# Small transposing products and one weight's join moved in the opening of a Fourier-mixing and gated feed-forward kernel

## The chip, the cores and the metric

The kernel runs on one core of one Trainium2 chip. The metric is the device time of one execution in microseconds. A core has a matrix engine (TensorE, PE in the profile) and three others that work on whole tiles: VectorE (DVE), ScalarE (ACT) and GpSimd (POOL). SyncE (SP) issues most DMA transfers. Each engine runs its own instructions strictly in order and waits on semaphores for the others.

## The reference

The input x has shape (8, 3008, 256). Its two-dimensional Fourier transform over sequence and features is taken, and the real part, as 24064 rows of 256, goes through a gated feed-forward layer:

```
X = fft(fft(x, axis=1), axis=2).real
gate = sigmoid(X @ w_gate)          # w_gate, w_val: 256 x 1536
out = (gate * (X @ w_val)) @ w_out  # w_out: 1536 x 256
```

The weights arrive as 64-bit floats.

## The kernel before

**Merged weights.** The transform over features is a fixed 256 x 256 matrix of cosines and sines (`dt`), so the kernel multiplies it into the two input weights once: `merge` (L335) makes G = dt x W. G has a cosine half G1 and a sine half G2. Row 0 of G2 is not a sine row but the row of the one middle frequency, and it is needed as a number per partition. So `ge_sums` (L351) transposes that row by products with a one-element matrix, 128 weights at a time, into the columns of one PSUM bank, and ACT copies the columns to `ge` (L360).

**Eighteen jobs.** The weights are cut in 18 jobs of 256 columns or rows. Jobs 0 to 11 alternate between gate and value weights (job 2c is gate, 2c+1 value, of column block c), 12 to 17 are of w_out. Each job is loaded (`weight_load`), its 64-bit numbers are taken apart on ACT (`weight_parts`, L301 and L302), put together as 32-bit numbers with three DVE instructions (L313, L314, L316, with a PSUM bank as scratch) and one POOL addition (L318, `weight_join`), and then used (`weight_use`): for jobs 0 to 11 four products on PE into a bank `ps`, which `merged` (L344) copies to G on ACT.

**Banks.** PSUM has eight banks. Three (`psx`) rotate among the merges of jobs 0 to 7 and the `pf` sums; five (`po0` to `po4`, NB = 5) are named by number through `bank(name, other)`. Whoever takes a bank waits until its last user's reads are done.

**The transform over the sequence.** For each of eight batches, rows are folded (on DVE for batch 0), then products with a cosine and a sine table (`st`) give sums `ev` and `od` of even and odd inputs for two blocks of frequencies. From them `half().then` (L511) copies `ev` to SBUF on ACT, and `places` (L526) writes sum and difference on DVE to the row tiles: `pk` for cosines, `qk` for sines. The sum fills the lower half of the frequencies from the start on, the difference the upper half from the end down. The middle feature's own row (`er`, `e0_sums`, `e0_copies`, `e0_row`) is spread to all partitions as `ek`.

**The main loop.** An iteration i (L1008) handles 128 of the 1536 inner columns for a chunk of 252 frequencies. Its sums lie in a bank `pf`: `seed` (ACT) writes ek x ge, `front_a` (PE) adds G1 x pk, `part` (ACT) copies twice that to `ae`, `front_b` (PE) adds G2 x qk. `gate_a` and `gate_b` (ACT and DVE) make sigmoid and product for a frequency and its mirror. `back` is the product with w_out; for the first chunk it goes straight to `rows` banks, later in a form with fewer products (`po`). Seeds rotate through the three `psx` banks, so a seed waits for the gate of three iterations before.

**The opening.** Ahead of the loop: PE is kept busy with products of ones (`warm`), jobs 0 to 7 are joined and merged, all their ge columns are made in one call (L895), batch 0 is folded and its cosine sums are taken (`cos`), the first three seeds, then jobs 8 and 9 are taken apart and joined (L918), and the sine sums (`sin`) alternate with the first three `front_a`. Jobs 8 to 17 are used inside the loop: the dictionaries `pre`, `mid` and `use` (L951 to L963) give, for each job, the iteration in which it is taken apart, joined and merged, and the iteration after that for its ge columns:

```
    for j, i in ((8, -2), (9, -1), (10, 0), (11, 1), (12, 2), (13, 4), ...
        ...
        use.setdefault(i + 2, []).append(lambda j=j: using(j))
        if jobs[j][0] < 2:
            use.setdefault(i + 3, []).append(lambda j=j: ge_sums((j,), (j + 1) % 2))
```

`using(j)` merges in bank `po` j % 2 and copies G at once. Inside an iteration the order is: front_a, gate_a, part, seed, gate_b (with `mid` in it), `pre`, `use`, back, front_b.

Of the kernel before, what the change touches and what calls it, by code (L numbers as in the profile page):

```python
# [12 lines left out]
ALU = mybir.AluOpType  # L13
# [69 lines left out]
def kernel(  # L83
# [10 lines left out]
    nc = tc.nc  # L94
    B, _, _, _, D = xf.shape
# [3 lines left out]
    M = S // 2  # L99
    NK = M + 1  # L100
    NE = (M // 2) // 2 + 1
    NO = (M // 2) // 2
    NFT = F // P
# [3 lines left out]
    NB = 1 + max(b // 3 for b in PLACE)  # L107
# [22 lines left out]
    op = ctx.enter_context(tc.tile_pool(name="op", bufs=1))  # L130
# [3 lines left out]
    def mm(o, l, r, start, stop):  # L134
        nc.tensor.matmul(o, l, r, start=start, stop=stop, skip_group_check=True)  # L135

    def bank(name, other=None):
        if other is not None:
            return pso.tile([P, 512], F32, name=name, tag=f"po{other}")
        return psx.tile([P, 512], F32, name=name, tag="x")  # L140
# [42 lines left out]
    ST = [const.tile([P, 2, NQ, NE + NO], F32, name="st", tag="st")]  # L183
# [3 lines left out]
    ge = const.tile([P, 2, NFT], F32, name="ge")  # L187
# [57 lines left out]
    jobs = [(w, c) for c in range(NPR) for w in range(2)] + [(2, c) for c in range(NPR)]  # L245
# [50 lines left out]
    def weight_parts(j):  # L296

        if j in RAW:
            raw, ws = RAW[j], WS[j]
            lo, hi = raw[:, :, :, 0], raw[:, :, :, 1]  # L300
            nc.scalar.activation(ws, hi.bitcast(F32), AF.Abs)  # L301
            nc.scalar.activation(lo, lo.bitcast(U32), AF.Copy, scale=2.0 ** -29)  # L302

    def weight_join(j, other=None):
        if j not in RAW:
            return
        raw, ws = RAW.pop(j), WS[j]
        lo, hi = raw[:, :, :, 0], raw[:, :, :, 1]
        wi = ws.bitcast(I32)
        mid_ = ws if other is None else bank("join", other).rearrange("p (c f) -> p c f", c=2)  # L310
        mi = mid_.bitcast(I32)
        ts = nc.vector.tensor_scalar
        ts(out=mid_, in0=ws, scalar1=2.0 ** -15, scalar2=HUGE, op0=ALU.max, op1=ALU.min)  # L313
        ts(out=mi, in0=mi, scalar1=3, scalar2=0x3FFFFFF8, op0=ALU.logical_shift_left,  # L314
           op1=ALU.bitwise_and)
        nc.vector.scalar_tensor_tensor(out=wi, in0=hi, scalar=-(2 ** 30), in1=mi,  # L316
                                       op0=ALU.bitwise_and, op1=ALU.bitwise_or)
        nc.gpsimd.tensor_tensor(wi, wi, lo, op=ALU.add)  # L318
# [3 lines left out]
    def weight_use(j, other=None):  # L322
        w, c = jobs[j]
        if w == 2:
            WO[c] = WS.pop(j)
            if c >= NPR - 2:
                lo = 2 * (c - NPR + 2)
                nc.sync.dma_start(out=wkeep[:, lo : lo + 2], in_=WO[c])
            for g in range(NG):
                if (3 * g + 2) // 2 == c:  # L330
                    parts_.extend(forms(g))
        else:
            merge(WS.pop(j), w, c, other)
# [10 lines left out]
    def merged(j):  # L344

        g, c = jobs[j]
        ps = MERGED.pop((g, c))
        cs = slice(c * WC, (c + 1) * WC)
        nc.scalar.copy(G[:, :, g, cs], ps.rearrange("p (h n) -> p h n", h=2))

    def ge_sums(js, other=None):  # L351

        ps = bank("ge", other)
        at_ = [(jobs[j][0], f) for j in js for f in range(2 * jobs[j][1], 2 * jobs[j][1] + 2)]
        for g, f in at_:
            mm(ps[:, g * NFT + f : g * NFT + f + 1], G2[0:1, g, f * P : (f + 1) * P], busy[0:1, 0:1],
               True, True)
        gs = sorted({g for g, _ in at_})
        lo, hi = min(f for _, f in at_), max(f for _, f in at_) + 1
        nc.scalar.copy(ge[:, gs[0] : gs[-1] + 1, lo:hi],  # L360
                       ps[:, 0 : 2 * NFT].rearrange("p (g f) -> p g f", g=2)[:, gs[0] : gs[-1] + 1, lo:hi])

    def forms(g):

# [122 lines left out]
    def half(b, w, d, blk, sn, other=None):  # L487


        c0, n = ((0, NE), (NE, 2 * NJ if b else NO))[blk]  # L490
        ev, od = [bank(name, other and other[i])[:, 0:n] for i, name in enumerate(("ev", "od"))]

        def sums(*qs):
            for q in sorted(qs, key=lambda q: q % 2):
                mm((ev, od)[q % 2], w(q), ST[0][0:NP, int(sn), q, c0 : c0 + n], q < 2, q >= NQ - 2)

        def both():

            for r in range(2):
                for q in range(N3):  # L500
                    for par, sum_ in enumerate((ev, od)):
                        rows = slice(par * HP, par * HP + HP - 1 - (par and q == N3 - 1))
                        if blk:
                            out_, wq = sum_[:, r * NJ : (r + 1) * NJ], q + N3 * r
                            tab = ST[1][rows, r ^ int(sn), q]
                        else:
                            out_, wq = sum_[:, r::2], q + N3 * (r ^ int(sn))
                            tab = ST[0][rows, int(sn), q, r:NE:2]
                        mm(out_, w(wq)[rows], tab, q == 0 and r == 0, q == N3 - 1)

        def then():  # L511
            a = evp.tile([P, 2 * NJ], F32, name="a", tag="a")
            if b and blk:
                for par, sum_ in enumerate((ev, od)):
                    f = a[:, par * NJ : (par + 1) * NJ]
                    nc.scalar.copy(f, sum_[:, 0:NJ])
                    for r, op_ in enumerate((ALU.add, ALU.subtract)):
                        nc.vector.tensor_tensor(ST[2][:, par, r::2], f[:, r : NJ - 1 + r],
                                                sum_[:, NJ + r : 2 * NJ - 1 + r], op=op_)
                return lambda: places(d, blk, sn, ST[2][:, 0], ST[2][:, 1])  # L520
            a = a[:, 0:n]
            nc.scalar.copy(a, ev)
            return lambda: places(d, blk, sn, a, od)
        return sums, then, both

    def places(d, blk, sn, ev, od):  # L526
        nc.vector.tensor_tensor(d[:, blk : blk + 2 * ev.shape[1] - 1 : 2], ev, od, op=ALU.add)
        lo, hi = (od, ev) if sn else (ev, od)
        top = M - blk
        nc.vector.tensor_tensor(d[:, top : top - 2 * NO + 1 : -2], lo[:, 0:NO], hi[:, 0:NO],  # L530
                                op=ALU.subtract)

    def whole(b, blk, what):
        _, then, both = seq_group(b, blk, what, (2, 3) if what else (0, 1))
# [8 lines left out]
    def seq_group(b, blk, what, other=None):  # L543
        return half(b, lambda q: W[b, blk][what][:, q, :], PQE[b][what], blk, what == 1, other)
# [33 lines left out]
    def e0_spread():  # L578

        ps = bank("ek", NB - 1)[:, 0:CH]  # L580
        mm(ps, busy[0:1, 0:P], shared["er"][:, 0:CH], True, True)
        EK[0] = ekp.tile([P, CH], F32, name="ek", tag="ek")
        nc.scalar.copy(EK[0], ps)
# [295 lines left out]
    def warm(n):  # L879

        ps = bank("warm", NB - 1)
        for _ in range(n):
            mm(ps[:, 0:CH], busy[:, 0:P], busy, True, True)

    shared["er"] = pqp.tile([P, NK + 1], F32, name="er", tag="pk")[0:1]
    warm(14)
    for j in range(8):
        weight_parts(j)
        if j > 2:
            merged(j - 3)  # L890
        weight_join(j, j % NB)
        weight_use(j)
    for j in range(5, 8):
        merged(j)
    ge_sums(range(8), 3)  # L895
    for j in range(N3):
        load_table(1, j)
    for j in range(8, KEEP):
# [11 lines left out]
        for sums, _, _ in cos:  # L910
            sums(2 * j, 2 * j + 1)
    put = [then() for _, then, _ in cos]
    for f in put:
        f()
    e0_spread()
    for i in range(N3):
        seed(i)
    for j in (8, 9):  # L918
        weight_parts(j)
        weight_join(j, NB - 1)  # L920
    sin = [seq_group(0, blk, 1, (2 * blk, 2 * blk + 1)) for blk in range(2)]

    def sines(j):
# [3 lines left out]
    def first(i):  # L927
        front_a(i)
        if i < 2:
            part(i)  # L930
# [3 lines left out]
    first(1)  # L934
    sines(2)
    first(2)
    for _, then, _ in sin:
        then()()
    for j in range(KEEP, len(jobs)):
        weight_load(j)  # L940
    nc.sync.dma_start(out=ed[0:1], in_=shared["er"])
# [9 lines left out]
    pre, use, mid = {}, {}, {}  # L951
    def using(j):
        weight_use(j, j % 2)
        if jobs[j][0] < 2:
            merged(j)
    for j, i in ((8, -2), (9, -1), (10, 0), (11, 1), (12, 2), (13, 4), (14, 6), (15, 8), (16, 10), (17, 12)):
        if i > 0:
            pre.setdefault(i - 1, []).append(lambda j=j: weight_parts(j))
        if i >= 0:
            mid.setdefault(i, []).append(lambda j=j: weight_join(j, 2))  # L960
        use.setdefault(i + 2, []).append(lambda j=j: using(j))
        if jobs[j][0] < 2:
            use.setdefault(i + 3, []).append(lambda j=j: ge_sums((j,), (j + 1) % 2))  # L963


    i0 = NFT
# [123 lines left out]
```

## Time and profile before

| What | Value |
|---|---|
| median of 3 runs | 1943.3 us (1940.19, 1943.3, 1943.42) |
| the profiled execution's own time | 1941.99 us |
| its span | 1940.2 us |
| PE busy | 1923.7 us, 99% of the span |
| DVE, ACT, POOL busy | 74%, 69%, 81% |
| last job joined ahead of the loop's own (job 9, DVE) | 51.67 us |
| first product of `front_b` | 54.80 us |
| first product of `rows` | 78.77 us |

A timeline line gives the start in the span, the time of the group, engine and line of the code, the operation, what it writes and reads, shapes, how many instructions were merged into the line, and in brackets the idle time ahead of it and what ended it. Every product is an instruction of helper line L135, so tiles tell them apart; a product of 32-bit numbers is two records, so four products show as x8. Ends of matmuls are modelled: the start of the next group is the better mark.

### The profile page before, as it was taken

How to read it: one execution, taken by the hardware profiler on the slowest of the kernel's cores; microseconds unless marked ns; L12 is line 12 of the kernel's file. 1: busy time of each engine (PE TensorE's matmuls, PEld its weight loads, DVE VectorE, ACT ScalarE, POOL GpSimd, SP SyncE). 2: the span in 40 equal slices, each digit the busy share in tenths (PEclk: the TensorE clock that was granted, in tenths of full speed). 3: DMA queues.
4: the chain of work that ended last, by engine and by line, in shares of the span. 5: the costliest groups of instructions: out<-in, count | busy, mean ns of one | idle time of the engine just before them, and what ended most of it. 6: DMA issues, size and time to landing. Idle time of an engine off the chain costs nothing.

```text
span 1940.2 us, 34490 instructions
## 1 busy us (share of the span) xinstructions
PE 1923.7 (99%) x11296; PEld 1793.6 (92%) x11296; DVE 1432.2 (74%) x3210; ACT 1347.6 (69%) x3151; POOL 1563.8 (81%) x2806
## 2 busy tenths in 40 slices
PE   9899999999999999999999999999999999999999
PEld 6799889999999999999999999999999999999998
DVE  7556787777777877778777786777777777776776
ACT  4677657776777677776777767777677776777775
POOL 2379989997889788986889878888789886777775
PEclk9999999999999999999999999999999999999999
DMA  9351422212022111312012021111200110011101
GB/s 293 119 109 30 113 60 67 52 23 79 15 52 55 37 57 20 71 31 79 17 35 69 14 81 26 47 47 22 83 17 15 21 21 14 15 19 22 25 17 30
DMA packets 165098, 97.87 MB, mean 50 GB/s; under 512 B 126298, under 2 KB 155068, under 8 KB 163128
## 3 DMA queue, kind: packets, MB, share of 16 engines
q1 hardware_dynamic: 164366, 95.17, 20.4%
q8 instruction: 91, 1.49, 0.3%
q14 instruction: 87, 0.71, 0.1%
q10 hardware_dynamic: 522, 0.50, 0.1%
q0 software_dynamic: 32, 0.00, 0.0%
HBM read 70.40 MB, written 47.24 MB: 61 GB/s over the span
## 4 chain that ended last, share of the span: by engine, by line
PE 95%; DVE 3%; ACT 1%; issue 0%; DMA 0%; POOL 0%; ACTq 0%; DVEq 0%
PE pf L135 49%; PE po L135 40%; PE ev L135 3%; PE rows L135 1%; PE od L135 1%; DVE c L819 1%; PE ps L135 1%; DVE z L679 0%; ACT pf L692 0%; PE row L135 0%; DVE join L314 0%; DVE h L691 0%; DVE h L695 0%; PE pe L135 0%; DVE join L313 0%
## 5 line engine op out<-in xcount | busy, mean ns | idle before, releaser
L701 POOL TENSOR_TENSOR sf<-h 128x168 f32<-128x168 f32 (+1 forms) x935 | 517.9, 573 | 213.1 <-DVE h L695 213.1
L701 POOL TENSOR_TENSOR sf<-h,sf 128x168 f32<-128x168 f32 (+1 forms) x1122 | 625.0, 577 | 58.1 <-DVE h L695 57.8
L135 PE MATMUL pf<-qk,G 128*128 128x252 f32 (+1 forms) x2304 | 583.0, 376 | 2.1 <-ACT ae L664 1.9
L135 PE MATMUL pf<-pk,G 128*128 128x252 f32 (+1 forms) x2304 | 582.8, 376 | 0.0
L695 DVE TENSOR_TENSOR h<-pf,z 128x252 f32<-128x252 f32 (+1 forms) x576 | 241.5, 419 | 428.2 <-ACT pf L692 428.2
L653 ACT ACTIVATE pf<-ek,ge 128x252 f32<-128x252 f32 (+1 forms) x1152 | 542.7, 471 | 18.9
L135 PE MATMUL po<-sf,wf 128*128 128x168 f32 (+1 forms) x2992 | 516.1, 305 | 0.0
L664 ACT ACTIVATE ae<-pf 128x504 f32<-128x504 f32 (+1 forms) x576 | 339.6, 590 | 233.2 <-PE pf L135 231.2
L135 PEld LDWEIGHTS pf<-pk,G 128*128 128x128 f32 x2304 | 436.3, 190 | 53.5 <-issue 1.6
L135 PEld LDWEIGHTS po<-sf,wf 128*128 128x128 f32 x2992 | 460.6, 190 | 8.1
L135 PE MATMUL po<-h,wf 128*128 128x168 f32 (+1 forms) x2618 | 463.2, 305 | 0.0
L819 DVE TENSOR_TENSOR c<-c 128x168 f32<-128x168 f32 (+1 forms) x929 | 437.9, 503 | 5.1
L135 PEld LDWEIGHTS pf<-qk,G 128*128 128x128 f32 x2304 | 410.9, 190 | 29.9 <-ACT ae L664 3.4
L135 PEld LDWEIGHTS po<-h,wf 128*128 128x128 f32 x2618 | 416.5, 190 | 16.2
L679 DVE TENSOR_TENSOR z<-ae,pf 128x504 f32<-128x504 f32 (+1 forms) x576 | 383.4, 666 | 42.1 <-ACT h L678 40.5
L678 ACT ACTIVATE h<-pf 128x252 f32<-128x252 f32 (+1 forms) x576 | 218.0, 378 | 161.8 <-PE pf L135 157.5
L692 ACT ACTIVATE pf<-z 128x252 f32<-128x252 f32 (+1 forms) x576 | 214.1, 372 | 89.0 <-DVE h L691 86.4
L691 DVE TENSOR_TENSOR h<-h,pf 128x252 f32<-128x252 f32 (+1 forms) x576 | 232.5, 404 | 0.0
L701 POOL TENSOR_TENSOR sf<-sf 128x168 f32<-128x168 f32 (+1 forms) x187 | 108.0, 578 | 14.7
L701 POOL TENSOR_TENSOR sf<-sf,h 128x168 f32<-128x168 f32 (+1 forms) x187 | 102.2, 546 | 0.0
L732 ACT COPY c<-po 128x504 f32<-128x504 f32 (+1 forms) x141 | 80.1, 568 | 0.0
L828 DVE STREAM_TRANSPOSE os<-c 128x256 f32<-128x256 f32 x184 | 70.7, 422 | 0.3 <-issue 0.3
(152 smaller groups left out, 919.7 us busy)
## 6 DMA issues: line engine op xcount, KB each, us to landing
x<-xr SPq DMA_DIRECT2D x14, 1536.0 KB
out_dram<-os SPq DMA_DIRECT2D x368, 56.0 KB
xr<-in_xf_dram SPq DMA_DIRECT2D x14, 768.0 KB
xr<-in_xf_dram SPq DMA_DIRECT2D x35, 256.0 KB
ek<-ed SPq DMA_DIRECT2D x39, 126.0 KB
out_dram<-os SPq DMA_DIRECT2D x284, 7.0 KB
st<-in_stab_dram SPq DMA_DIRECT2D x6, 658.9 KB
x<-in_xf_dram SPq DMA_DIRECT2D x3, 1024.0 KB
```

Source lines behind the costliest of these rows:

```text
L135: nc.tensor.matmul(o, l, r, start=start, stop=stop, skip_group_check=True)
L653: nc.scalar.activation(PF[i][:, g], EK[i // NFT], AF.Copy, scale=ge[:, g, f : f + 1])
L664: nc.scalar.activation(AP[i], PF[i], AF.Copy, scale=2.0)
L678: nc.scalar.activation(H[p][:, fh, 0:n], PF[i][:, 0], AF.Sigmoid)
L679: nc.vector.tensor_tensor(z[:, :, ::-1], AP.pop(i), PF[i], op=ALU.subtract)
L691: nc.vector.tensor_tensor(h[:, fh, 0:n], h[:, fh, 0:n], pf[:, 1], op=ALU.mult)
L692: nc.scalar.activation(pf[:, 0], z[:, 0], AF.Sigmoid)
L695: nc.vector.tensor_tensor(h[:, fh, n:], pf[:, 0], z[:, 1], op=ALU.mult)
L701: nc.gpsimd.tensor_tensor(block(p, dst), block(p, a), block(p, b), op=(ALU.subtract, ALU.add)[op])
L732: (nc.vector.tensor_copy if t == 1 or t == 3 and not last else nc.scalar.copy)(C[0][:, 3 * t * R : 3 * (t + 1) * R], PO[t][:, 0 : 3 * R])
L819: engine.tensor_tensor(t[:, dst * R : (dst + 1) * R], *v, op=(ALU.subtract, ALU.add)[op])
L828: nc.vector.transpose(os_[0][:, s, 0:nb, h, :], t[:, c0 : c0 + nb * TB])
```

## The change

Four edits, all in the first 75 us or so:

- `ge_sums` is split: it makes the products into a bank that may be handed in, and a new `ge_out` makes ACT's copy. The ge products of jobs 0 to 5 go into bank po3 one job at a time, between the merges of jobs 3 to 7, with one copy; those of jobs 6 and 7 go to bank po4 in iteration 0, behind the merge of job 8.
- The joins of jobs 0 to 7 use three banks instead of five, and there are 12 warm products instead of 14.
- `places` can do its lower or its upper part alone (argument `high`). For batch 0, both blocks' lower parts come first, then both upper parts. The join of job 9 moves behind all four of the sines' parts; it used to stand ahead of the sine sums.
- In the loop, jobs 8 to 11 are merged in iterations 0, 2, 3, 4 (before: 0, 1, 2, 3), each with its ge one iteration later, in banks po3, po4, po3 and po0 (before: the bank `(j + 1) % 2`, which is the one that the next merge uses).

The order of instructions changes on PE, DVE and ACT. On POOL and SP it stays.

```diff
-    def ge_sums(js, other=None):
-
-        ps = bank("ge", other)
-        at_ = [(jobs[j][0], f) for j in js for f in range(2 * jobs[j][1], 2 * jobs[j][1] + 2)]
-        for g, f in at_:
+    def ge_at(js):
+        return [(jobs[j][0], f) for j in js for f in range(2 * jobs[j][1], 2 * jobs[j][1] + 2)]
+
+    def ge_sums(js, other, ps=None):
+
+        ps = bank("ge", other) if ps is None else ps
+        for g, f in ge_at(js):
             mm(ps[:, g * NFT + f : g * NFT + f + 1], G2[0:1, g, f * P : (f + 1) * P], busy[0:1, 0:1],
                True, True)
...
+        return ps
+
+    def ge_out(js, ps):
+        gs, fs = [sorted({a[i] for a in ge_at(js)}) for i in range(2)]
+        to = slice(gs[0], gs[-1] + 1), slice(fs[0], fs[-1] + 1)
+        nc.scalar.copy(ge[:, to[0], to[1]],
+                       ps[:, 0 : 2 * NFT].rearrange("p (g f) -> p g f", g=2)[:, to[0], to[1]])
...
+    def places(d, blk, sn, ev, od, high=None):
+        if not high:
+            nc.vector.tensor_tensor(d[:, blk : blk + 2 * ev.shape[1] - 1 : 2], ev, od, op=ALU.add)
+        if high in (None, 1):
...
-    warm(14)
+    warm(12)
+    ges = None
     for j in range(8):
         weight_parts(j)
         if j > 2:
             merged(j - 3)
-        weight_join(j, j % NB)
+        weight_join(j, j % 3)
+        if j == 7:
+            merged(5)
+            ge_sums((4, 5), None, ges)
         weight_use(j)
-    for j in range(5, 8):
+        if 2 < j < 7:
+            ges = ge_sums((j - 3,), 3, ges)
+    ge_out(range(6), ges)
+    for j in (6, 7):
         merged(j)
-    ge_sums(range(8), 3)
...
     put = [then() for _, then, _ in cos]
-    for f in put:
-        f()
+    for high in range(2):
+        for f in put:
+            f(high)
...
     for j in (8, 9):
         weight_parts(j)
-        weight_join(j, NB - 1)
+    weight_join(8, NB - 1)
...
-    for _, then, _ in sin:
-        then()()
+    put = [then() for _, then, _ in sin]
+    for high in range(2):
+        for f in put:
+            f(high)
+    weight_join(9, NB - 1)
...
-        use.setdefault(i + 2, []).append(lambda j=j: using(j))
-        if jobs[j][0] < 2:
-            use.setdefault(i + 3, []).append(lambda j=j: ge_sums((j,), (j + 1) % 2))
+        if jobs[j][0] == 2:
+            use.setdefault(i + 2, []).append(lambda j=j: using(j))
+    for j, i, other in ((8, 0, 3), (9, 2, 4), (10, 3, 3), (11, 4, 0)):
+        use.setdefault(i, []).append(lambda j=j: using(j))
+        use.setdefault(i + 1, []).append(lambda j=j, other=other: ge_out((j,), ge_sums((j,), other)))
+    use[0].append(lambda: ge_out((6, 7), ge_sums((6, 7), 4)))
```

More of the change, by code (lines that the diff above doesn't have):

```diff
@@ L349, in merged @@
         nc.scalar.copy(G[:, :, g, cs], ps.rearrange("p (h n) -> p h n", h=2))
-    def ge_sums(js, other=None):
-        ps = bank("ge", other)
-        at_ = [(jobs[j][0], f) for j in js for f in range(2 * jobs[j][1], 2 * jobs[j][1] + 2)]
-        for g, f in at_:
+    def ge_at(js):
[3 more added lines that the diff above has]
+        for g, f in ge_at(js):
             mm(ps[:, g * NFT + f : g * NFT + f + 1], G2[0:1, g, f * P : (f + 1) * P], busy[0:1, 0:1],
                True, True)
[L358 to L361, printed above, removed]
+        return ps
[4 more added lines that the diff above has]
+                       ps[:, 0 : 2 * NFT].rearrange("p (g f) -> p g f", g=2)[:, to[0], to[1]])
     def forms(g):
@@ L519, in then @@
                                                 sum_[:, NJ + r : 2 * NJ - 1 + r], op=op_)
-                return lambda: places(d, blk, sn, ST[2][:, 0], ST[2][:, 1])
+                return lambda *a: places(d, blk, sn, ST[2][:, 0], ST[2][:, 1], *a)
             a = a[:, 0:n]
             nc.scalar.copy(a, ev)
-            return lambda: places(d, blk, sn, a, od)
+            return lambda *b_: places(d, blk, sn, a, od, *b_)
         return sums, then, both
[L526 to L531, printed above, removed]
+    def places(d, blk, sn, ev, od, high=None):
+        if not high:
+            nc.vector.tensor_tensor(d[:, blk : blk + 2 * ev.shape[1] - 1 : 2], ev, od, op=ALU.add)
+        if high in (None, 1):
+            lo, hi = (od, ev) if sn else (ev, od)
+            top = M - blk
+            nc.vector.tensor_tensor(d[:, top : top - 2 * NO + 1 : -2], lo[:, 0:NO], hi[:, 0:NO],
+                                    op=ALU.subtract)
     def whole(b, blk, what):
```

## The prediction

> **What bounds the kernel now.** I read the page's head first, then the chain of waits, then each engine's timeline over the first 80 us, where alone the two instruction orders differ (POOL and SP keep theirs; from the first `rows` product on PE's order is the same too).
>
> ```profile
> span 1940.2 us, 34490 instructions
> PE 95%; DVE 3%; ACT 1%; issue 0%; DMA 0%; POOL 0%; ACTq 0%; DVEq 0%
> ```
>
> PE carries 95% of the chain, so a microsecond that PE gains before `rows` and that nothing later absorbs is a microsecond of the span. PE's timeline (start, us, group, what it waited for):
>
> ```profile
> 26.36 3.73 PE L135 MATMUL ge<-busy,G 1*128 1x1 f32 x32
> 30.02 1.11 PE L135 MATMUL pe<-st,x 126*1 126x377 f32 x8
> ...
> 54.80 1.01 PE L135 MATMUL pf<-qk,G 128*128 128x252 f32 x4
> 55.74 0.60 PE L135 MATMUL ge<-busy,G 1*128 1x1 f32 x4
> 59.21 1.96 PE L135 MATMUL ps<-raw,dt 128*128 128x256 f32 x8 [2.87 <-ACT ge L360]
> 61.01 1.01 PE L135 MATMUL pf<-qk,G 128*128 128x252 f32 x4
> 61.95 0.60 PE L135 MATMUL ge<-busy,G 1*128 1x1 f32 x4
> 64.13 3.37 PE L135 MATMUL ps<-wc,dt 128*128 128x256 f32 x8 [1.58 <-ACT ge L360]
> ...
> 72.60 1.96 PE L135 MATMUL ps<-wc,dt 128*128 128x256 f32 x8 [2.58 <-ACT ge L360]
> ```
>
> There is one solid block of ge products, 3.66 us from its start to the next group's, and later three idle stretches, 2.87 + 1.58 + 2.58 = 7.03 us, each a merge waiting for ACT's copy of the previous ge out of the same bank. `rows` starts at 78.77. ACT's timeline shows the other anchor:
>
> ```profile
> 47.92 0.67 ACT L301 ACTIVATE raw<-raw 128x512 f32<-128x512 f32 x1 [0.18 <-DMA raw<-in_moe_w_val_dram]
> 48.50 0.67 ACT L302 ACTIVATE raw<-raw 128x512 int32<-128x512 uint32 x1
> 49.06 0.57 ACT L664 ACTIVATE ae<-pf 128x504 f32<-128x504 f32 x1
> ```
>
> Weight 9 lands at 47.9, and ACT does nothing behind it earlier. The DMA queue is full until then; the change moves no DMA issue ahead of it.
>
> **The change, step by step.**
>
> *Two warm products fewer, three join banks instead of five: 0.* Warming would end 0.85 us earlier (4 passes of 0.21), but the merges are fed by POOL every 2.06 us, and by the fourth (15.26) PE already waits for POOL. The joins of one bank follow each other on DVE anyway.
>
> *The first ge products between merges: PE 3 us earlier at 27, worth 0 by 50.* Now 4 passes (0.46 by the block's rate, 3.66/32) follow merges 3, 4, 5 and 6, and 8 passes (0.92) come ahead of merge 7. The merges take 1.78 back to back. From merge 3 at 15.26 (1.93 to the next group): 17.2, and with three more pairs of merge and ge 17.65, 19.9, 22.1 to 24.4; ge of jobs 4 and 5 to 25.3; merge 7 to 27.1. POOL's join 7 (end 24.39) is hidden. So the first `pe` starts at 27.1 instead of 30.02. ACT has one copy more (0.17, cover: it idles 2.42 ahead of its last G copy). But the third part of x reaches DVE at 31.80 and its sums are ready at 36.0, so the last cosine group starts at 36.1 instead of 39.35, `ek` at 38.8 instead of 42.07. The reordered cosine places cost here: the sines' first od product waits for the place that frees its bank,
>
> ```profile
> 42.86 0.53 DVE L530 TENSOR_TENSOR pk<-a,od 128x376 f32<-128x376 f32 x1
> ```
>
> which now stands behind the other block's lower one (its copy ends at 39.6): 40.6 instead of 40.0, 0.6 lost. First pf product 42.6 instead of 45.45. Then ACT meets weight 9 at 47.92 as before: `part` at 49.06 and 49.55, the sines' copies at 50.05 and 50.45 (before 50.52 and 51.78, held by PE).
>
> *The sines' places ahead of join 9: +0.7 at the first qk product.* On DVE the join of weight 9 ran from 49.46 to 51.67. Now DVE idles from 49.4 until the copy (50.56), does four places in 1.85, and only then the join: 52.4 to 54.55 (three of 0.73). On POOL its addition is late by as much and passes nothing; join 10 ends at 56.6 instead of 55.55. On PE the last pf of the opening ends at 50.3, merge 8 starts when POOL has weight 8 (50.8; before 53.07) and ends at 52.75. The ge of jobs 6 and 7 is next, and its bank is the one join 9 works in: PE stands idle **1.85 us**, until 54.6. With 0.92 for the eight passes the first qk product starts at 55.5 instead of 54.80. Were join 9 still early, the lower places would end at 53.0 as before and the first qk product, behind ge, could start at 53.7: this part by itself costs 1.8.
>
> *Merges one step earlier, ge in banks of their own: -8 us from there to rows.* From the first qk product to `rows` took 78.77-54.80 = 23.97. PE's work in it is 8 pf groups of 0.85, three merges of 1.78, four ge of 0.46: 14.0. The rest was the 7.03 of waits, 1.7 of a half-clock stretch (below), and 1.2 of refills. Now the merge follows the next qk product and waits for POOL only (56.0, 58.0, 61.5; all hidden), and each ge waits for G copied a step before. What is late next is ACT: h at 56.6, `part` 57.75, sigmoid 58.25, weight 12's two conversions to 59.7, h at 59.75; DVE's second h product of group 0, behind join 11, ends at 60.4; only then may ACT seed the bank again (0.97): 61.45. So the first new pf starts at 61.5 with PE free at 60.35: 1.15 idle. Later the ge of job 10 waits 0.5 for G behind weight 13's conversions. Otherwise PE runs: 62.8 merge 10, 64.6, 65.4, 67.3 merge 11, 69.1, 69.9, ge, `rows` at **71.3**; I add 0.2 for weight loads that the tiny groups expose (0.09 at 55.74). 71.5 against 78.77 is -7.3.
>
> *Clock.* The windows over PE show the granted clock:
>
> ```profile
> 63.00:64.00 1.00, 0.00 (x0) 1.00 0.00 0
> 64.00:65.00 1.00, 0.87 (x3) 0.77 0.00 0
> 65.00:66.00 1.00, 1.00 (x3) 0.50 0.06 16
> 66.00:67.00 1.00, 1.00 (x4) 0.50 0.00 0
> ```
>
> Half clock came twice, 30.4 to 33.8 after the ge block, 64.5 to 67.9 after waits, 3.4 us each; the stretch of 3.4 us before each held at most about a third of dense products. The new stretch 52.75 to 55.5 holds none, so a half-clock stretch after it is likely (2 in 3, since its place varies). It slows 1.8 us of work by double up to 61.5, where 1.15 is idle: about 0.3 of it gets through (0 to 1.7).
>
> [...]
>
> **Sum.** The profiled execution's own time is 1941.99 (its span and 1.8 around it): -7.3 + 0.3 gives **1935.0**. It lies 1.3 below the median of 1943.3, so against that the sum is -0.43%. Bounds: tiny passes at 0.15 (0.60/4) instead of 0.114 in the main loop give +0.4; no new waits (1.85 + 1.15 + 0.5) -3.5, but the seeds tie the second, so -2.4 at most; a full half-clock stretch +1.4; the three runs lie from 1.8 below to 1.4 above that own time.
>
> **Rivals.**
> 1. *ACT takes the place of the waits* (12%). Its seeds, conversions and copies fill each step; if each of the three steps still holds PE by the smallest old wait (1.58 instead of my 1.65 in all), 3 x 1.58 - 1.65 = +3.1: 1938.1. For it: 61.5 is set by ACT. Against: PE's work per step (3.94) is over ACT's 3.7.
> 2. *The waits stay under other names* (8%): the ge products waited for their copy only because ACT came late; G's copy is as late. The sum loses all but the half-clock: 1941.99 + 0.7 - 1.7 = 1941. Against it: the merge was released by the ge copy in all three rows.
> 3. *The late join decides* (6%): join 9 ends 2.9 later (54.55 for 51.67). If joins 10 to 12 and the gates behind them on DVE carry this on, and the old waits remain, the merges are late by 2.9, the eight ge passes in front of the first qk product come on top (0.92), and the longer gap brings another half-clock stretch (1.7): 1941.99 + 5.5 = 1947.5, slower than before. It decides from the point where join 10 (56.6) ends after the first h (57.04): now 0.4 short of it.
> 4. *The clock stays full* (part of the forecast's 74%): 1934.7.
>
> **Chances.** Forecast with or without the half clock 74%, rivals 12, 8, 6. A measurement here tells 0.2%, 3.9 us, from no change; faster means under 1939.4. Forecast and rival 1 lie there, but for 0.03 in their tails: 0.83; same holds rival 2, these tails and a milder rival 3: 0.12; slower the rest of rival 3: 0.05. The range goes from 1931.9 (own time's low run and the waits in part) to 1939.0, past rival 1; it leaves out the rest.
>
> **What would show it.** `pe` at 27 rather than 30; 6 ge copied before the last G; the first qk product near 55.5 behind ge that waited for DVE's join; no `ps` waiting for ACT's ge; `rows` at 71 to 72, and the same duration from there to the end. Wrong if the ge of jobs 6 and 7 is not held by the join (then about 2 less), or if `rows` is later than 75.

## The result and the profile after

| | before | after |
|---|---|---|
| median | 1943.42 us (5 runs, 1940.19 to 1947.12) | 1934.58 us (5 runs, 1934.3 to 1937.33) |
| the profiled execution's own time, its span | 1941.99, 1940.2 us | 1937.33, 1935.5 us |
| first `pe` product | 30.02 us | 27.96 us |
| first qk product | 54.80 us | 55.84 us |
| first `rows` product | 78.77 us | 74.06 us |

The ratio of the times on record is 0.9958, with a 95% interval of 0.9943 to 0.9973: faster by 0.42% (the two medians divided give 0.9955). 1935.0 was predicted. Three executions of one experiment (own banks, below) took 2415, 3393 and 6060 us, the first two at mean granted clocks of 0.78 and 0.56; they are left out.

The profiles place the whole difference ahead of `rows`: it starts 4.71 us earlier, the span is 4.7 shorter. The profiled execution is the slowest of the five after, so this is less than the 8.8 between the medians. This is PE's timeline of the kernel after.

```profile
24.61 1.49 PE L135 MATMUL ge<-busy,G 1*128 1x1 f32 x12
26.04 1.99 PE L135 MATMUL ps<-wf,dt 128*128 128x256 f32 x8
27.96 0.81 PE L135 MATMUL pe<-st,x 126*1 126x377 f32 x8
...
51.10 1.99 PE L135 MATMUL ps<-wf,dt 128*128 128x256 f32 x8 [0.17 <-POOL wf L318]
54.87 1.05 PE L135 MATMUL ge<-busy,G 1*128 1x1 f32 x8 [1.77 <-DVE raw L316]
55.84 1.12 PE L135 MATMUL pf<-qk,G 128*128 128x252 f32 x4
56.89 0.88 PE L135 MATMUL ge<-busy,G 1*128 1x1 f32 x4
57.71 2.05 PE L135 MATMUL pf<-qk,G 128*128 128x252 f32 x4
59.55 3.62 PE L135 MATMUL ps<-raw,dt 128*128 128x256 f32 x8
...
65.75 1.99 PE L135 MATMUL ps<-wc,dt 128*128 128x256 f32 x8
...
69.90 1.99 PE L135 MATMUL ps<-wc,dt 128*128 128x256 f32 x8
...
74.06 1.99 PE L135 MATMUL rows<-wc,h 128*128 128x256 f32 x8
```

The three idle stretches of 2.87, 1.58 and 2.58 ahead of `ps` are gone. In their place stands one wait of 1.77 at the ge products of jobs 6 and 7, on the last DVE instruction of join 9. Merge 9 (59.55) takes 3.62 instead of 1.99: the windows over PE of the same kernel show half clock there (columns: window, length, PE busy and count, granted clock, DMA share, GB/s).

```profile
56.00:57.00 1.00, 1.00 (x5) 1.00 1.05 389
57.00:58.00 1.00, 1.00 (x5) 0.53 0.54 186
...
63.00:64.00 1.00, 1.00 (x4) 0.55 0.00 0
64.00:65.00 1.00, 1.00 (x7) 1.00 0.00 0
```

The granted clock in the rows at 57 and 63 (0.53 and 0.55) puts it from 57.06 to 63.9. The chain of waits of the kernel after, from 30 to 80 us, tells what sets the start of all this:

```profile
35.66 12.45 DMA raw<-in_moe_w_val_dram
...
49.43 0.95 ACT ae L671 x2
50.38 0.37 ACT a L527
...
51.78 0.92 DVE qk L537 x2
52.70 0.61 DVE join L313
...
54.12 0.70 DVE raw L316
54.83 0.04 issue
54.87 1.05 PE ge L135 x8
```

Weight 9's transfer, ACT's two `part` and two copies, DVE's places, join 9, and only then PE. PE's earlier finish of the opening is not on it.

### The profile page after: what moved, and what is told of

Same layout as the page of the kernel before. It is cut to its first block, busy times and chain, and to the rows that moved or that the text cites. A ratio compares the mean times of both kernels' runs of the same rounds, so it can differ in the third digit from the quotient of the medians.

```text
span 1935.5 us, 34483 instructions
## 1 busy us (share of the span) xinstructions
PE 1924.0 (99%) x11292; PEld 1793.3 (93%) x11292; DVE 1435.0 (74%) x3210; ACT 1346.7 (70%) x3152; POOL 1561.6 (81%) x2806
## 4 chain that ended last, share of the span: by engine, by line
PE 94%; DVE 2%; DMA 2%; ACT 1%; SPq 0%; issue 0%; ACTq 0%; DVEq 0%
PE pf L135 49%; PE po L135 40%; PE ev L135 2%; PE rows L135 1%; DMA st<-in_stab_dram 1%; DVE c L826 1%; DMA raw<-in_moe_w_val_dram 1%; PE od L135 1%; DMA wf<-in_moe_w_val_dram 1%; DVE z L686 0%; PE ps L135 0%; PE row L135 0%; ACT pf L699 0%; DVE h L702 0%; DVE h L698 0%; SPq L294 0%
```

## The experiments

Times are medians, each with its ratio to the kernel before on the same chip and the 95% interval.

### The ge products in banks of their own, alone

```diff
-            use.setdefault(i + 3, []).append(lambda j=j: ge_sums((j,), (j + 1) % 2))
+            use.setdefault(i + 3, []).append(lambda j=j: ge_sums((j,), (3, 4, 3, 0)[j - 8]))
```

> The kernel before with one thing changed: in the loop, the ge products of jobs 8 to 11 go to banks po3, po4, po3 and po0 instead of the bank that the next merge takes. Steps, opening and join 9 stay as before. My theory (the merge waited for ACT's ge copy only because it wanted that bank): no ps waits for a ge copy; merge 9 starts at 56.2 right behind the ge of job 8; the seeds of the fourth pf on ACT end at 60.9; rows starts near 70 instead of 78.8, so 1933 to 1935 us, as good as the whole change, without its later steps. Rival (the waits stay under other names, since G's copy is as late on ACT as ge's): PE waits at ge for G's copy instead, rows at 76 to 78, 1940 to 1942 us.

> The same kernel as own_banks, for a profile at full clock. Expected as there: no ps waits for a ge copy, merge 9 near 56.2, rows near 70, 1932 to 1934 us; rival: PE waits at ge for G's copies, rows at 76 to 78, 1940 us.

> The same kernel as own_banks, for a profile at full clock, which the first two looks did not give. Expected as there: merge 9 near 56.2 behind the ge of job 8, no ps waits for a ge copy, rows near 70 to 71.5, 1932 to 1935 us. Rival: PE waits at ge for G's copies, rows at 76 to 78, 1940 us.

Measured three times, with four executions counted of each: medians of 1934.4, 1934.45 and 1933.85 us, ratios 0.9958 (0.9944 to 0.9972), 0.9945 (0.9931 to 0.9958) and 0.9951 (0.9938 to 0.9965). The third profile, of an execution of 1932.17 us, is at full clock in all of the opening. PE's timeline of it:

```profile
53.26 1.01 PE L135 MATMUL pf<-qk,G 128*128 128x252 f32 x4
54.21 0.60 PE L135 MATMUL ge<-busy,G 1*128 1x1 f32 x4
54.74 1.99 PE L135 MATMUL ps<-raw,dt 128*128 128x256 f32 x8
56.57 1.01 PE L135 MATMUL pf<-qk,G 128*128 128x252 f32 x4
58.09 0.60 PE L135 MATMUL ge<-busy,G 1*128 1x1 f32 x4 [0.51 <-ACT G L349]
58.63 1.99 PE L135 MATMUL ps<-wc,dt 128*128 128x256 f32 x8
...
68.98 1.89 PE L135 MATMUL rows<-wc,h 128*128 128x256 f32 x8
```

No `ps` waits for a ge copy; of the waits under other names only 0.51 us is left (ge of job 9 on G's copy). From the first qk product to `rows` it takes 15.72 us, where the kernel before took 23.97. The rival falls: choosing another bank for eight tiny products holds the whole gain. Where the mean granted clock is 1.0 it holds more than that: the three such executions here took 1931.99 to 1932.17 us, the three such of the kernel after 1933.94 to 1934.58, so there the rest of the change costs about 2 us. Over all executions the medians are level; nine of the twelve here have a mean clock of 0.999 or 0.998.

### The loop's part alone

Banks as above, and merges 9 to 11 one step later as in the change; opening and join 9 as before.

```diff
-        use.setdefault(i + 2, []).append(lambda j=j: using(j))
-        if jobs[j][0] < 2:
-            use.setdefault(i + 3, []).append(lambda j=j: ge_sums((j,), (j + 1) % 2))
+        if jobs[j][0] == 2:
+            use.setdefault(i + 2, []).append(lambda j=j: using(j))
+    for j, i, other in ((8, 0, 3), (9, 2, 4), (10, 3, 3), (11, 4, 0)):
+        use.setdefault(i, []).append(lambda j=j: using(j))
+        use.setdefault(i + 1, []).append(lambda j=j, other=other: ge_sums((j,), other))
```

> The kernel before with the loop's part of the change alone: banks po3, po4, po3, po0 and the merges of jobs 9 to 11 one step later; the block of ge products in the opening and the early join 9 stay. My theory (the loop's part holds the whole gain, the opening's gain is absorbed by the landing of weight 9): first qk product at 54.8, rows at 70.5 to 71, 1934 us, within 1 us of the whole change. Rival (the opening's part is needed): 3 us more than the whole change, 1937 to 1938 us.

Measured: 1934.01 us, ratio 0.996 (0.9947 to 0.9972), as the whole change. The rival (1937 to 1938) falls: all five executions lie between 1933.91 and 1935.73. In its profile half clock runs from 29.5, at the end of the block of ge products, to 36.3 (an `ev` takes 1.46 at 34.59 and 0.79 at 38.90), the first qk product comes only at 56.45, and `rows` at 72.41: 15.96 us from one to the other.

### The opening's part alone

```diff
...
-        weight_join(j, j % NB)
+        weight_join(j, j % 3)
+        if j == 7:
+            merged(5)
+            ge_sums((4, 5), None, ges)
         weight_use(j)
...
+        if 2 < j < 7:
+            ges = ge_sums((j - 3,), 3, ges)
...
+        if j == 8:
+            use[0].append(later_ge)
...
```

> The kernel before with the opening's part alone: ge products of jobs 0 to 5 between the merges in bank po3 with three join banks, those of jobs 6 and 7 behind merge 8 in bank po4; join 9 early, cosine and sine places in the old order, later ge in the bank of the next merge as before. My theory: the first pe product starts at 27 to 28 instead of 30.0, ACT still meets weight 9 at 48 and the first qk product starts at 53.9 instead of 54.8; the three waits for the ge copies stay at about 7 us in sum; 1941 to 1942.5 us. Rival (the 3 us of the opening get through): first qk product at 51.8, 1939 us.

Measured: 1942.47 us, ratio 1.0 (0.9991 to 1.0009). The first `pe` starts at 27.93, the first qk product at 52.98, 1.8 earlier than before; weight 9 was on ACT at 47.16 here. The waits of this kernel's PE between 50 and 85 us:

```profile
PE ps L135 <- ACT ge L365: 7.3, 3, 3.2
```

They are as before, 7.3 us in three. No gain in the time can be measured: the rival's 1939 is excluded, the theory's range is met, and the interval allows a gain of 0.09%, 1.7 us. The profiled execution (1945.73) had half clock in three places between 55 and 79 us, so it can't tell whether the 1.8 us get through. Executions with the same mean granted clock can: at 0.998 three of the kernel before on this chip have a median of 1941.80 and seven of this one 1941.79, at 0.996 two have 1944.68 and three 1944.61. So nothing of the opening's 2 us is seen in the time. If the 1.8 of the profile are typical, they are lost between the first qk product and `rows`; which wait takes them is not shown.

### Join 9 ahead of the sine sums again

```diff
     weight_join(8, NB - 1)
+    weight_join(9, NB - 1)
...
-    weight_join(9, NB - 1)
```

> The kernel after, with the join of job 9 ahead of the sine sums' places again, as it was before the change. My theory (the new wait of 1.8 us on PE is the ge of jobs 6 and 7 behind join 9, and the gates behind joins 9 and 10 on DVE are late with it): ge starts right behind merge 8 near 53.1, the first qk product at 54.0 instead of 55.8, the first z on DVE at 55.8, rows 1.6 us earlier where the clock is alike, 1932.5 to 1933.5 us. Rival (the places come later by as much as the join comes earlier, so the first qk product gains nothing): 1934.5 us as after.

Measured: 1933.06 us (1932.75 to 1933.75), ratio 0.9953 (0.994 to 0.9967). PE's timeline of its profile:

```profile
50.70 1.89 PE L135 MATMUL ps<-wf,dt 128*128 128x256 f32 x8
52.52 1.05 PE L135 MATMUL ge<-busy,G 1*128 1x1 f32 x8
53.50 1.12 PE L135 MATMUL pf<-qk,G 128*128 128x252 f32 x4
...
59.90 1.12 PE L135 MATMUL pf<-pk,G 128*128 128x252 f32 x4 [1.13 <-ACT pf L660]
...
69.89 1.99 PE L135 MATMUL rows<-wc,h 128*128 128x256 f32 x8
```

The new wait is gone: ge follows merge 8 at once. From merge 8 to the first qk product it takes 2.80 us, against 4.74 in the profile after and 4.02 in a later one of the same kernel at full clock; from merge 8 to `rows` 19.19, against 20.41 in the latter. So at full clock 1.2 us of PE's time hang on the place of join 9, and in the profiles the rival (no gain at the first qk product) falls. The median lies 1.5 and 1.0 below the two medians of the kernel after; the ratios' intervals overlap, so the times alone don't decide it.

### Join 9 in another bank, still late

```diff
-    weight_join(9, NB - 1)
+    weight_join(9, 2)
```

> The kernel after with join 9, still behind the sines' places, in bank po2 instead of po4, so that the ge of jobs 6 and 7 does not wait for it. My theory (two things hold PE, the bank and the place of the join in DVE's order): first qk product at 54.0 instead of 55.8, but the first z waits on DVE behind joins 9 and 10 until 56.9, so the seeds and rows gain only 0.5 us: 1934.0 us. Rival (the bank is all): as join9_early, 1933.0 us.

Measured: 1934.72 us (1933.94 to 1936.1), ratio 0.9949 (0.9937 to 0.9962). DVE's timeline of this kernel:

```profile
53.71 0.69 DVE L316 SCALAR_TENSOR_TENSOR raw<-raw,join 128x512 int32<-128x512 int32 x1
54.51 0.69 DVE L313 TENSOR_SCALAR join<-wc 128x512 f32<-128x512 f32 x1
55.23 0.70 DVE L314 TENSOR_SCALAR join<-join 128x512 int32<-128x512 int32 x1
55.97 0.70 DVE L316 SCALAR_TENSOR_TENSOR wc<-wc,join 128x512 int32<-128x512 int32 x1
56.57 0.68 DVE L686 TENSOR_TENSOR z<-ae,pf 128x504 f32<-128x504 f32 x1
```

PE no longer waits at ge and starts the first qk product at 54.20, but z follows joins 9 and 10 without a gap, not the sigmoid that PE releases. (With join 9 early, z idled 1.80 for that sigmoid.) The next new pf then waits 1.56 for its seeds (61.04), where 1.13 was seen with the join early. So part of the wait moved one place on: from merge 8 to `rows` it takes 19.62, between the 19.19 with the join early and the 20.41 of the kernel after at full clock. That is the theory's mechanism; in the times no gain over the kernel after can be measured.

### The old steps with the early join

```diff
-    for j, i, other in ((8, 0, 3), (9, 2, 4), (10, 3, 3), (11, 4, 0)):
+    for j, i, other in ((8, 0, 3), (9, 1, 4), (10, 2, 3), (11, 3, 0)):
```

> join9_early with the merges of jobs 9 to 11 in the steps of before (one step earlier than in the change), the ge products still in banks of their own. If the later steps are worth nothing and a merge ahead of the next qk product only fills PE while ACT gets the seeds ready: first qk product at 53.5, merge 9 behind the ge of job 8 at 55, first new pf at 61.4, rows at 68.5 to 69, 1931.5 to 1932.5 us, below join9_early's 1933.06. Rival (the later steps were needed, since G's copy and the ge products behind it come too late in the old ones): rows at 71 or later, 1934 us or more.

Measured: 1932.77 us (1931.99 to 1933.91), ratio 0.9939 (0.9926 to 0.9951). In its profile weight 9 came 1 us later than in the profile of before, the first qk product at 54.72 and `rows` at 70.83: 16.11 us, against 16.39 with the later steps. The ge of job 9 does wait for G's copy, as the rival had it, but only 0.80 us. The absolute times of the expectation were missed by 1 to 2 us with the landing; all five executions lie below the rival's 1934. The later steps are not needed, and what the old ones gain over join 9 early can't be told from nothing.

### The gap filled, and the kernel after once more

```diff
+    def dense():
+        ps = bank("warm", 1)
+        for _ in range(4):
+            mm(ps[:, 0:CH], busy[:, 0:P], busy, True, True)
+    use[0].append(dense)
     use[0].append(lambda: ge_out((6, 7), ge_sums((6, 7), 4)))
```

> The kernel after with four dense products of ones (1.7 us, into bank po1, read by nobody) ahead of the ge of jobs 6 and 7, where PE waits 1.77 us for join 9. Theory (the stretch without dense products brings the half clock and this is the 2 to 3 us by which executions of the same kernel differ): ge starts no later than 54.9, no half clock between 52 and 72, all five executions within 0.5 us of 1934.5. Rival (the clock falls for another reason): half clock in the profile's rows again or executions at 1936 and more as before.

Measured: 1934.54 us, ratio 0.9951 (0.9938 to 0.9965). Its profile has full clock from 52 to 72, but one execution of five took 1938.39. The theory's "all within 0.5 us" fails: that execution has a mean granted clock of 0.998, as the rival had it.

> The kernel after once more, for its spread: three of its five executions lay within 0.3 us of 1934.4 and two at 1936.4 and 1937.3. Expected if the half clock behind the new gap is what adds 2 to 3 us: again some at 1934.3 to 1934.6 and some at 1936 to 1937.5, none between 1932 and 1934. Rival (another source of spread): values spread evenly.

Measured: 1934.07 us, ratio 0.9954 (0.9941 to 0.9968); four executions from 1933.94 to 1934.08, one of 1935.38. Neither expectation as written: no value near 1937, and the odd one lies in between. The profile, of 1933.94, has full clock throughout the opening although the wait at ge is there. PE's timeline of it:

```profile
53.16 1.05 PE L135 MATMUL ge<-busy,G 1*128 1x1 f32 x8 [1.16 <-DVE raw L316]
54.14 1.12 PE L135 MATMUL pf<-qk,G 128*128 128x252 f32 x4
...
60.55 1.12 PE L135 MATMUL pf<-pk,G 128*128 128x252 f32 x4 [1.13 <-ACT pf L660]
...
70.53 1.99 PE L135 MATMUL rows<-wc,h 128*128 128x256 f32 x8
```

From the first qk product to `rows`: 16.39 us here, 18.22 in the profile after. So the half clock cost the profiled execution of the result 1.8 us; the other 1.7 of the 3.5 between the two `rows` lies ahead of the qk product, where weight 9 came 3.1 us earlier here.

The mean granted clocks on record bear on whether the new wait makes the half clock likelier. At 0.998 an execution spent some 6 to 10 us at half clock, by estimate from the rounded mean (twice 0.0015 to 0.0025 of 1934 us). Five of the ten executions of the kernel after are there, one of the five with the gap filled, and none of the fifteen of the three kernels in which PE doesn't wait for join 9 (join 9 early, in another bank, old steps). That points to the wait; where the stretches lay is known only for the profiled executions.

## Why the prediction was right, and where it was off

**Size and cause were right.** 1935.0 against a median of 1934.58. The -8 was put on the span from the first qk product to `rows`; from 23.97 it was to fall to 16.0, and 16.39 was measured in the kernel after at full clock. Its cause was put on the shared bank together with the moved merges; own banks (15.72) and the old steps (16.11) show that the bank alone holds it. That the absolute time fits to 0.4 us is in part luck: the ten executions of this kernel spread from 1933.94 to 1937.33.

**Warm products and join banks: 0.** The first merge starts at 8.99 instead of 9.85, and the fourth at 15.32, beside 15.26. As predicted; no run tries the join banks or the warm products by themselves.

**The opening: 3 us that are worth 0 by 50.** `pe` came 2.06 earlier, not 2.9. The term was mis-sized: a merge between tiny groups takes 1.92 to the next start instead of 1.78, and four tiny passes take 0.53 instead of 0.46 (17.25 to 17.78). That it is worth nothing in the time is shown by the opening's part alone. The reason given, the landing of weight 9, is shown only in part: it is on the chain of after, but in the opening's part alone the first qk product came 1.8 earlier with weight 9 only 0.76 earlier, so about 1 us passed that anchor and yet did not reach the time. Nor is the landing a constant: ACT took up weight 9 between 45.1 and 48.9 in ten profiled executions, nine times right after its landing. The absolute positions behind it (54.6, 55.5) agree with the profile after by luck of the landing, its 48.20 beside 47.92.

**The cosine places' order.** In the profile after, the od product waited 0.55 for the place that frees its bank; 0.6 was predicted. In the later profile of the same kernel no such wait is listed.

**Join 9.** A wait of 1.85 was predicted, 1.77 and 1.16 were measured. That this part by itself costs 1.8 fits the profile after (from merge 8 to the first qk product 4.74 against 2.80 with the join early) and is too high for the later one (4.02) and for the medians (1.0 to 1.5). What varies is the wait: in the later profile merge 8 starts 0.98 earlier, but join 9 ends 1.70 earlier, so PE waits less for it. The seeds take nothing of it back: they hold PE for 1.13 with the join early and late alike, where 1.15 was predicted, and from the first qk product to `rows` both take 16.39. Only in the other bank do they wait longer, 1.56.

**Words.** The prediction's heading calls the merges one step earlier. Those of jobs 9 to 11 come one step later; its working used the later places.

**The half clock** was the term that was mis-sized: a stretch of 3.4 us, likely in two of three executions, with 0.3 us getting through. In the profiled execution it lasted 6.8 us, longer than the slack, and 1.8 got through. How often it comes was about right: five of the ten executions of the kernel after have a mean clock of 0.998. Its price was not: two of these five took 1934.3 and 1934.41, no more than those at 1.0, and three took 1935.38 to 1937.33, of which a part can be the landing. The median execution had a mean clock of 1.0 and stands beside the 1934.7 of the prediction's fourth rival. In the profile after, the half clock at 57.06 followed a gap of 1.77, twelve tiny passes and one group of qk products; that such a mix brings it was the prediction's estimate, and no run shows it.

**Rivals.** ACT did take a place, but once (1.13 at the seeds, which the forecast had) and not three times. Waits under other names measured 0.51 in own banks; in the kernel after none is listed, not even the 0.5 predicted for the ge of job 10. The late join cost what is said above and did not turn the sign.

## What to carry to other kernels

Where a wait names a tiny copy, ask first which buffer the waiting instruction wants: here the choice of banks for eight tiny products holds the gain, and the elaborate rest of the change adds nothing that can be measured, and costs about 2 us where the clock is full. Before crediting work moved out of an opening, find what the engine waits for behind it, a transfer above all, and measure the opening alone: here 2 us gained at its end are not seen in the time. And when a filler is moved to the end of another engine's queue, follow the bank it works in as well as its place in the order.

## What the runs showed of the hardware

The spread between the executions of own banks comes in steps. The twelve counted lie at 1932.0 to 1932.2 (mean granted clock 1.0), 1933.6 to 1934.0 (0.999) and 1935.2 to 1935.4 (0.998): 1.5 to 1.7 us apart. In the profile of the kernel before the half clock lasts 3.4 us each time (30.40 to 33.81 and 64.53 to 67.95), in the profile after 6.8 us (57.06 to 63.9). A stretch like those of before would cost a PE that is the bound half its length, 1.7 us, by estimate. A lower mean clock did not always come with a longer time: of the executions of the kernel after, one of 1934.3 had 0.998, one of 1934.58 had 1.0.

It is not the code alone that decides on such stretches. They came at the end of the block of ge products in some executions (at 30.40 in the kernel before and 29.5 in the loop's part alone, where the block starts at 26.36 and 26.39 and the first `ev` behind it takes 1.63) and not in others (own banks, the third profile, with the same block at 26.48: the first `ev` takes 0.90). The wait for join 9 is no different: behind 1.77 of it the half clock began at 57.06 in the profile after, and behind 1.16 of it the later profile of the same kernel kept a granted clock of 1.00 from 54 to 61. Which property of the work ahead of a stretch brings it is not shown.
